# A new order and new engine choices for the tasks of an attention-then-SwiGLU kernel

## The chip, the cores and the metric

The kernel runs on one core of a Trainium2 chip. The metric is the device time of one execution in microseconds (us). Of the kernel before there are four timed executions, 257.27 to 258.35 us, with a median of 257.82 us, and one profiled execution of 259.26 us.

The core has a matrix engine (PE; its weight loads are listed as PEld), a vector engine (DVE), a scalar engine (ACT), a general engine (POOL) and a queue engine (SP), which issues the DMAs here. Each engine works through its own list of instructions in order. An instruction that needs another engine's result waits for it, and everything behind it on its engine waits too.

## The reference

```
# q, k, v: (4 batches, 8 heads, 768 positions, 64); heads 0, 2, 6 are "retrieval" heads
scores = q @ k^T / 8
retrieval heads: causal mask
other heads:     causal, and (key < 4  or  query - key < 64)
a = softmax(scores);  x = (a @ v), heads put side by side      # 3072 x 512
g = x @ w_gate;  silu = g / (1 + exp(-g))
out = (silu * (x @ w_val)) @ w_out                             # d_ff = 1536, float32
```

## The kernel before

The 3072 rows are 24 tiles of 128 queries. Tile t belongs to a pair n = t // 2, and a pair (256 positions of one batch, all heads) is what is loaded together: `load q n`, `load k n` and `load x n` (x is v), 512 KB each. The weights come in 18 loads of 512 KB: `load g n`, `load v n`, `load o n` with n from 0 to 5 for w_gate, w_val and w_out. All land as float32 in a ring of 14 buffers ("raw") and are cast to float16 by the tasks `cq`, `ck`, `cx` and `wc g`, `wc v`, `wc o` on ACT, DVE or POOL.

For pairs 0 to 4, q and k are turned on PE (`tr n.0` for q, `tr n.1` for k, lines 435 and 438) and copied out of PSUM by `evq` and `evk`. From pair 5 on, DMAs do that (`dq`, `dk`, lines 416 and 422). `fill3` clears the buffer that these DMAs read for q.

Each tile t then runs through: scores `sc t.u` on PE (line 547, one unit u after another through one PSUM buffer of two banks), exponentials `ex t.u` on ACT (line 557), and for tiles 4 and up a multiplication of units 0 and 1 by a 0/1 mask, `mask t.u`, on DVE or POOL (line 565; unit 0 has 128x1024 elements, unit 1 has 128x640). Then the values `val t.1` and `val t.0` on PE (line 577), and the division by the row sums, `nm` (lines 582 and 594). `sk` and `sv` copy the first four keys and values of a batch into other blocks. The tile is turned by PE (`xtr`, copied out by `xe`) for tiles 0 to 7, by a DMA (`xdma`, line 604) from tile 8 on.

Four tiles make a group g for the second half. For each of 12 slices j of d_ff, `gate g.j` and `vals g.j` (line 778, four matmuls each; the first four slices of group 0 are cut into two halves of columns, named .0 and .256) write to a ring of three PSUM banks ("gv"). `tanh` on ACT (line 784), `stt1` (line 788) and `stt2` (line 795) on DVE make h from them; `stt1` frees the gate's bank, `stt2` the value's bank. Slices 2n and 2n+1 need `wc g n` and `wc v n`. The output `out g.tt.third` (line 813) goes through one PSUM bank for groups 0 to 4, is copied out by `oe`, and stored by `st`.

All of that is recorded as a list of tasks, in the code's own order, with what each depends on. What is issued, and in which order, is written out by hand in two strings. `ORDER` holds two characters per task, a number in base 62: a number below 3700 is the index of a task in that list, and 3700 + k stands for k matmuls of a dummy product, `warm(k)` (line 292). `WAYS` holds one digit per task: which of the engines that the task allows is taken. Since every engine works in order, `ORDER` fixes each engine's list, SP's list of DMAs among them, and which PSUM or SBUF buffer is free for whom.

```
numbers = [DIGITS.index(ORDER[2 * i]) * 62 + DIGITS.index(ORDER[2 * i + 1]) ...]
for t, w in zip(self.tasks, WAYS):
    t.way = t.ways[int(w)]
...
for number in P.order():
    if number < P.FILL:
        P.tasks[number].run()
    else:
        warm(number - P.FILL)
```

Of the kernel before, what the change touches and what calls it, by code (L numbers as in the profile page):

```python
# [13 lines left out]


ORDER = (
    "000802041L1M1T091O1V1Nxl1Y1W1U1Z1X1a0A01xj1b1c0B1p1t1q0C1Q0E1R1P1r031f0D1d2527262D280i1u1s1S1y2G"
    "0j2j1g2E1exi1i1h1n2H1o212I2F1j2A1k1l1v221z2J2K1w1x201mxh2L2M23290F24xh2p2N2O2P2q2V2W2r2Q2R102B9F"
    "2C2S9G159j2X2Z9Z2a112k0p2s169k2b9H0H2t2Y2c2d9a9b9P2x9l2e2T2y3Q9m9c2U2h9n0o2u2i9Q2v369R0I0k9o9d9p"
    "05063W3Y0G133A129q9I9J9S9T3B0q9r9s3D073X3E9K9L9M3R3Z3a9N30319e3C0K189O9t3M3b9f9y0n2w2m2l9u9g9v3c"  # L20
    "329h3e33192z9zA0A10L499i3F349U2o354F0t3f2n3G0l0JA29w1H2fAN3d9V3p0m9W4A4G4H9x3H1I0s3h37AO3IAS3J3i"
    "383KAT3t3u9XAP394I3L9YAQ4J3j3k1B3SA83N3V4K0r0M3O3g3TAR3lAV1E3m4L0NAUA9AA3zAW3n3oAI403wAJAD3xA30O"
    "3P41421F3q3U3v43AK443r3sALAEAFAM0v4NA41C3y45461K4WA54p4O4qAG4oAHA60PA747480yAB4Z4yBk4a2gACBlBmBn"
    "4PBVBoBWBG4c4wAwBXBHBI4d0xAzAx4Q4RAyB00u4BBfBgBhBiBjBJBK4M4C4S4TBQBR4xB6B7BS4v0w4f4gAu4E0zB8BTAr"
    "0R4l4DAs4z5014BUAtB1B24U4V0S17AX4YAv52Ba53Bb4uB31D1ABYAY0Y4b4e4X5D1G4r4h5758B90QBZ4i5G1JAZ5W5X5Z"
    "4jAaBABLB45e515H5JBM5V5K544kBc0TAc4mB5BB555IAdAe5f4s59BN5LBC56BO5M5N5cAf5d0U5A5BAhAi5O5P5C5E4t5Y"
    "5Q5RBEBPAg5g635F5S5h5iAjAk5r4nBDBd0X5T5U62615a5s5tAmAnAoBFCd5b6iAbCeAp6ABeCgCfCh69CYCZCOBpCPCQ5o"
    "5y6B68Aq0WBqBrCa5jBsCRCS5p6F6GC9CbCcCA5k5qBuCB0V0a6C6DCs6O6HBvCt6X6Y5uCu6h6l6gAl6m5vCvCw6UCiBt66"
    "6V6o6p5l6n5m64CjCkCl6q6E6RCJ6SCK6d5w5xCLCECm6I6J6TBw655n5zD26K0h8d600ZCT7PBx7XByBzCF6WD30b6u6v67"
    "6LC07W6MD46P6NCMCUCNCV6Q6r6sC16Z6aC2C3D5CHD66x6y6bCG6eCW757TCICx6cCX7879Cn7OCC6j6k7BC46t71Cy0gC5"  # L30
    "C6C7CzCDD0Co726fEA0d7C7N7V7UEBD7Cp0cCqCr6z70D1C8D86w737AEF747v8283EC7REGEH7g7hE0E57jE6E17tE27u7k"
    "D9DAEIEJE77D767I7J0f7SEDEEE8E97Q7EDgDR7FDhDSDT7GDCDD7H7YE37K7L0e7Z8a8h7lDEDiDbDeE481DcDU807i7q87"
    "7mDdDFDG88EKDH7nDV8YDy77DI7a7bDfDJDvDK7cELEMDLDw847o7pDMDxDq858A8B7rDW8G7z8c8MDNDO8Z8NDz7s7MDrDs"
    "DPDtDu868P8i7dDjDk7eDX8fDZ8QDYDa7w8JENEODl7x8gDm8CEPDnDo7fFSDpFTDB8D8KFU8V89FIFJ8EF3FL8pFKEyFMEz"
    "F0EQERES8H8F8eF1F88qF28OF9FA8mFDFEF4EU8L7y8R8S8nEVETF5DQFVFW8j8xF6F78kEW8lEX8r8s8T8U8WFGFFFH8oFc"
    "FdFNFOFP93948IEZEaFf8b8tEY8u90FeFg8X91EtEuEbEcEvFQ8vFB8w8z8y92EwFC989A99FXExFY969BEeFZ97Eo95Ep9C"
    "Fa9D9EFbEfEqEgEhFRErEsEjEkEmElEnGuGvGwGBGxGyFhGGGHGIEiGCGDGkGlGmFiGnGoFjGEGFGQFkGRGsFmFnGpGSEdGq"
    "GrGtFoFpFqG1G2GVGWG4G3G5G6GXFrFsGYGZGaGbGcFtFuGJGKG7GLGMFwFlG8FvG9GdGAFxGTGNGeGUGOGPGfFyGgFzGhGi"
    "GzH0GjH1G0H4H5H6H9HAHBHEHFHGH7H2H3H8HCHDHJHHHIHKHL"
)  # L40
WAYS = (
    "000000000000000000000000000000000000000000000000000000000000002022222222222222222210201212101000"
    "011000000100000000000000010001100202212210110100100001000000000000000200022220001101000000000000"
    "020000000000000010012220220000000100000000000100000000100000000012210220110000100000000011000100"
    "000000021010210210000000000000000002000010000000000002200120000000100000000001000010001210200000"
    "001001000000200001000000000000222020100000010010000000021000000100000000020122000000001000000000"
    "010000210020002200000000010000000200010000000000101222022000000100000000000000001000000000000000"
    "000000000000000000000000000000000000000000000000000000000000000000000000000000000000010000000000"
    "000000000000000000000000000000000000000000000000000000000000000010000000001000000000000000000000"
    "000000000000000000000000000000000000000000000000000000000000000000000000000000000000000000000000"  # L50
    "000000000000000000000000000000001000000000100000000000000000000000000000000000000000000000000000"
    "000000000000000010000000000000000000000000000000000000000000000000000000000000000000000000000000"
    "10000000000000000010"
)
# [878 lines left out]
```

## Time and profile before

| | |
|---|---|
| median of four timed executions | 257.82 us |
| the profiled execution, its own time | 259.26 us |
| its span, first to last instruction | 257.1 us |
| mean granted clock of the matrix engine | 0.999 |
| PE busy | 247.3 us, 1813 matmuls |
| DVE busy | 167.6 us, 344 instructions |
| ACT busy | 139.3 us, 230 instructions |
| POOL busy | 97.3 us, 124 instructions |
| read from HBM, written to it | 28.31 MB, 6.29 MB |
| 128x512 matmul, four of them in a row | 0.86 us |
| mask 128x1024 on POOL, mean of both forms there | 1.88 us |
| mask on DVE, mean of both forms there | 0.74 us |
| exponential 128x1024 on ACT | 1.02 us |
| `stt1`, `stt2` on DVE, mean | 0.655 us |

The span is shorter than the time by 2.2 us, which lie before the first and after the last instruction. Busy time of PE counts a matmul from its start to its modelled end, so overlapping matmuls look longer than their share: a 128x512 matmul is listed with 368 ns, and yet four of them follow each other in 0.86 us.

### The profile page before, as it was taken

To read this page: it belongs to the slowest core of one execution; us is meant where nothing else is said; L and a number is where in the kernel's file an instruction comes from. 1 tells how busy PE (TensorE), PEld (TensorE's weight loads), DVE (VectorE), ACT (ScalarE), POOL (GpSimd) and SP (SyncE) were. 2 spreads that over 40 slices of the span, in tenths; PEclk is the share of its full clock that TensorE was granted. 3 is DMA by queue.
4 is the path that set the end of the run, shared out by engine and by line. 5 is a ranking of instruction groups with operands and counts; after the bars stand their busy time and mean duration, and the time that the engine had idled before them with its cause. 6 is when DMAs were issued, how large, how long until landed. Compare 5 with 4: busy or idle time off the path is not lost.

```text
span 257.1 us, 4866 instructions
## 1 busy us (share of the span) xinstructions
PE 247.3 (96%) x1813; PEld 136.8 (53%) x1813; DVE 167.6 (65%) x344; ACT 139.3 (54%) x230; POOL 97.3 (38%) x124
## 2 busy tenths in 40 slices
PE   7988988999999999999999999999999999999994
PEld 3666755765555564555655555555455554444442
DVE  3577999899869482588865637476665856455610
ACT  2876997776566664376655753564545323133101
POOL 6474689665661644263620821412142200000000
PEclk9999999999999999999999999999999999999999
DMA  7999999976958989997999972362222122031034
GB/s 186 290 320 317 318 324 333 288 248 157 323 148 204 224 161 192 236 220 158 223 231 233 182 163 55 70 129 59 60 56 50 20 55 49 0 83 41 16 94 97
DMA packets 80535, 42.52 MB, mean 165 GB/s; under 512 B 32768, under 2 KB 76032, under 8 KB 80512
## 3 DMA queue, kind: packets, MB, share of 16 engines
q1 hardware_dynamic: 80352, 42.09, 68.4%
q8 instruction: 14, 0.23, 0.4%
q10 hardware_dynamic: 160, 0.13, 0.2%
q14 instruction: 9, 0.07, 0.1%
HBM read 28.31 MB, written 6.29 MB: 135 GB/s over the span
## 4 chain that ended last, share of the span: by engine, by line
PE 78%; DVE 9%; SPq 5%; DMA 4%; ACT 2%; issue 1%; POOL 0%; DVEq 0%
PE gv L778 42%; PE o_ps L813 23%; PE sc L547 7%; PE av L577 4%; SPq L317 4%; DMA raw<-in_k_dram 4%; DVE h L795 2%; DVE e L565 2%; DVE vt L181 1%; DVE sil L788 1%; DVE xb L594 1%; SPq L325 1%; DMA out_dram<-o_sb 1%; ACT e L557 1%; ACT qT L175 1%
## 5 line engine op out<-in xcount | busy, mean ns | idle before, releaser
L557 ACT ACTIVATE e<-sc 128x1024 f16<-128x1024 f32 (+3 forms) x71 | 62.3, 880 | 35.3 <-PE sc L547 35.1
L778 PE MATMUL gv<-xt,wg_sb 128*128 128x512 f16 (+1 forms) x304 | 72.6, 368 | 1.0 <-POOL hq L177 0.6
L778 PE MATMUL gv<-xt,wv_sb 128*128 128x512 f16 (+1 forms) x304 | 72.6, 368 | 0.4 <-DVE sil L788 0.3
L813 PE MATMUL o_ps<-wo_sb,h 128*128 128x512 f16 (+2 forms) x300 | 70.0, 371 | 0.0
L788 DVE SCALAR_TENSOR_TENSOR sil<-sig,gv 128x512 f32<-128x512 f32 (+1 forms) x76 | 49.3, 655 | 30.9 <-ACT sig L784 30.1
L784 ACT ACTIVATE sig<-gv 128x512 f32<-128x512 f32 (+1 forms) x76 | 43.0, 575 | 48.5 <-PE gv L778 47.4
L795 DVE SCALAR_TENSOR_TENSOR h<-sil,gv 128x512 f16<-128x512 f32 (+1 forms) x76 | 49.2, 655 | 15.0 <-PE gv L778 13.8
L565 POOL TENSOR_TENSOR e<-e,m 128x1024 f16<-128x1024 f16 (+1 forms) x19 | 35.8, 1882 | 42.0 <-ACT e L557 37.7
L813 PEld LDWEIGHTS <-h 128*128 128x128 f16 x300 | 28.2, 98 | 28.4
L778 PEld LDWEIGHTS <-wg_sb 128*128 128x128 f16 x304 | 28.6, 98 | 27.6 <-issue 1.6
L778 PEld LDWEIGHTS <-wv_sb 128*128 128x128 f16 x304 | 28.4, 98 | 27.1 <-issue 0.9
L547 PE MATMUL sc<-qT,kT 128*128 128x256 f16 (+1 forms) x276 | 37.5, 257 | 0.1
L547 PEld LDWEIGHTS <-kT 128*128 128x128 f16 x276 | 25.2, 98 | 14.8 <-DVE kT L177 0.8
L577 PEld LDWEIGHTS <-e 128*128 128x128 f16 x472 | 19.8, 97 | 9.2 <-DVE e L565 1.7
L577 PE MATMUL av<-vt,e 128*128 128x65 f16 x472 | 22.5, 193 | 1.5 <-DVE e L565 0.7
L175 ACT COPY o_sb<-o_ps 128x512 f32<-128x512 f32 (+1 forms) x17 | 9.8, 579 | 20.5 <-PE o_ps L813 20.5
L594 DVE TENSOR_TENSOR xb<-av,rc 128x256 f16<-128x256 f32 x45 | 19.1, 424 | 1.5
L582 DVE RECIPROCAL rc<-av 128x4 f32<-128x4 f32 x48 | 8.6, 178 | 14.7 <-PE av L577 14.2
L177 POOL CAST vt<-raw 64x512 f16<-64x512 f32 x22 | 14.3, 651 | 9.3 <-DMA raw<-in_v_dram 8.4
L177 POOL CAST hq<-raw 128x1024 f16<-128x1024 f32 (+1 forms) x14 | 12.9, 927 | 10.5 <-DMA raw<-in_k_dram 6.8
L565 DVE TENSOR_TENSOR e<-e,m 128x640 f16<-128x640 f16 (+1 forms) x19 | 14.0, 740 | 0.2 <-ACT e L557 0.2
L177 DVE COPY o_sb<-o_ps 128x512 f32<-128x512 f32 (+1 forms) x8 | 5.1, 639 | 13.4 <-DMA out_dram<-o_sb 10.7
(55 smaller groups left out, 135.6 us busy)
## 6 DMA issues: line engine op xcount, KB each, us to landing
raw<-in_q_dram SPq DMA_DIRECT2D x12, 512.0 KB, 6.5
raw<-in_k_dram SPq DMA_DIRECT2D x12, 512.0 KB, 7.2
raw<-in_v_dram SPq DMA_DIRECT2D x12, 512.0 KB, 7.1
out_dram<-o_sb SPq DMA_DIRECT2D x46, 128.0 KB, 2.4
raw<-in_moe_w_gate_dram SPq DMA_DIRECT2D x6, 512.0 KB, 7.5
raw<-in_moe_w_val_dram SPq DMA_DIRECT2D x6, 512.0 KB, 8.1
raw<-in_moe_w_out_dram SPq DMA_DIRECT2D x6, 512.0 KB, 5.3
xt<-xb SPq DMA_TRANSPOSE x16, 2.5
```

The lines of the kernel that those rows point to most:

```text
L175: nc.scalar.copy(out=dst, in_=src)
L177: ENG[task.way].tensor_copy(out=dst, in_=src)
L547: nc.tensor.matmul(sc[c // 4][:, c % 4:c % 4 + n, :], weights, moving, start=first, stop=last)
L557: nc.scalar.activation(out=e[:, 0:n], in_=whole_sc.pop((t, u))[:, 0:n], func=AF.Exp, scale=scale)
L565: ENG[task().way].tensor_tensor(out=ev, in0=ev, in1=mm, op=ALU.mult)
L577: nc.tensor.matmul(av[:, n, 0:65], ee, vv, start=(m == 0), stop=(m == len(bl) - 1))
L594: nc.vector.tensor_tensor(out=xbs[t][:, :, odd, :], in0=av[:, :, 0:64], in1=rc.to_broadcast([128, 4, 64]), op=ALU.mult)
L778: nc.tensor.matmul(ps, wsb[:, kk, j * 128:(j + 1) * 128], xt[:, kk, c[0]:c[1]], start=(kk == 0), stop=(kk == 3))
L784: nc.scalar.activation(out=sg[g, j, c], in_=gs[g, j, c], func=AF.Tanh, scale=0.5)
L788: nc.vector.scalar_tensor_tensor(out=sl[g, j, c], in0=sg.pop((g, j, c)), scalar=1.0, op0=ALU.add, in1=gs.pop((g, j, c)), op1=ALU.mult)
L795: nc.vector.scalar_tensor_tensor(out=hs[g, j][:, c[0]:c[1]], in0=sl.pop((g, j, c)), scalar=0.5, op0=ALU.mult, in1=vs.pop((g, j, c)), op1=A ...
L813: nc.tensor.matmul(o_open[g, tt, x], hs[g, j][:, tt * 128:(tt + 1) * 128], wo_sb[:, j, lo:hi], start=(j == 0), stop=(j == NJ - 1))
```

## The change

The change replaces both strings and nothing else. The tasks, what they compute and what they depend on stay. Cut to its first lines:

```diff
 ORDER = (
-    "000802041L1M1T091O1V1Nxl1Y1W1U1Z1X1a0A01xj1b1c0B1p1t1q0C1Q0E1R1P1r031f0D1d2527262D280i1u1s1S1y2G"
...
+    "080400091L1O021M1N01xh1T1U1W1V1Xxi1Y1a1Z1K0B0A1Rxm1t1u25261P0C280E031Q2D1r2G1S1s271n1d1o1b2E2j2I"
...
 WAYS = (
-    "000000000000000000000000000000000000000000000000000000000000002022222222222222222210201212101000"
...
+    "000000000000000000000000000000000000000000000000000000000000002020222122002102002000012221100010"
...
```

Decoded, the engines' lists differ from place to place. PE's list from its start:

```diff
-warm(10) tr0.0 warm(5) tr0.1 warm(3) sc0.0 sc1.1 sc1.3 sc1.2 val0.1 sc0.1 tr1.0 val1.0 warm(2) val0.0
-sc1.0 tr1.1 xtr0 val1.1 warm(1) sc2.0 xtr1 warm(1) tr2.0 val2.1 sc3.0 val2.0 gate0.0.0 gate0.3.0 sc3.1
-val3.1 gate0.2.0 tr2.1 ...
+warm(10) warm(1) tr0.0 warm(2) tr0.1 warm(6) sc1.3 tr1.0 sc1.2 sc1.0 sc0.1 sc0.0 tr1.1 val0.0 val0.1
+sc1.1 sc2.0 val1.0 tr2.0 val1.1 sc3.0 warm(1) val2.1 xtr0 sc3.1 val3.1 xtr1 warm(1) val2.0 tr2.1
+gate0.2.0 ...
```

SP's list of DMAs from its start:

```diff
-q0 k0 x0 q1 k1 q2 x1 g0 g1 k2 v1 q3 v0 k3 g2 x2 v2 q4 g5 k4 v5 g3 x3 g4 v4 v3 x4 q5 k5 o1 x5 o4
-dk5.1 dq5.1 o3 o0 dk5.0 dq5.0 o2 o5 k6 x6 xdma8 ...
+q0 k0 q1 x0 k1 q2 x1 k2 g1 g0 v1 q3 v0 k3 g2 x2 v2 q4 g5 v5 g4 v4 x3 g3 k4 q5 v3 k5 x4 q6 o3
+dq5.0 dk5.0 dq5.1 dk5.1 k6 o2 o1 o4 o0 o5 xdma8 dk6.1 x5 ...
```

128 tasks go to another engine. By engine, the tasks whose numbers change:

| tasks | before | after |
|---|---|---|
| masks | DVE 19, POOL 19 | DVE 22, POOL 16 |
| casts of q and k | ACT 9, DVE 5, POOL 21 | ACT 6, DVE 7, POOL 22 |
| casts of v | ACT 16, DVE 10, POOL 22 | ACT 12, DVE 12, POOL 24 |
| casts of the weights | ACT 1, POOL 19 | ACT 8, DVE 2, POOL 10 |
| copies of turned k | ACT 3, DVE 4 | ACT 1, DVE 6 |
| copies of the output | ACT 17, DVE 8 | ACT 14, DVE 11 |
| divisions | ACT 3, DVE 45 | ACT 1, DVE 47 |
| copies of turned x | ACT 2, DVE 6 | ACT 1, DVE 7 |
| `fill3` | POOL | DVE |
| dummy matmuls on PE | 22 | 21 |

Of the first masks, 4.0 and 5.0 go from DVE to POOL, 6.0 from POOL to DVE, 6.1 and 7.0 from DVE to POOL; 4.1 and 5.1 stay on DVE and 7.1 on POOL. The two casts of the first q (`cq0.0`, `cq0.1`), which stood on ACT and POOL, both stand on ACT. Of the w_out casts, 1 and 3 go to DVE, 2, 4 and 5 to ACT, and 0 stays on POOL.

More of the change, by code (lines that the diff above doesn't have):

```diff
@@ L16 @@
 ORDER = (
-    "000802041L1M1T091O1V1Nxl1Y1W1U1Z1X1a0A01xj1b1c0B1p1t1q0C1Q0E1R1P1r031f0D1d2527262D280i1u1s1S1y2G"
[L18 to L36, printed above, removed]
@@ L37 @@
-    "Fa9D9EFbEfEqEgEhFRErEsEjEkEmElEnGuGvGwGBGxGyFhGGGHGIEiGCGDGkGlGmFiGnGoFjGEGFGQFkGRGsFmFnGpGSEdGq"
-    "GrGtFoFpFqG1G2GVGWG4G3G5G6GXFrFsGYGZGaGbGcFtFuGJGKG7GLGMFwFlG8FvG9GdGAFxGTGNGeGUGOGPGfFyGgFzGhGi"
-    "GzH0GjH1G0H4H5H6H9HAHBHEHFHGH7H2H3H8HCHDHJHHHIHKHL"
+    "080400091L1O021M1N01xh1T1U1W1V1Xxi1Y1a1Z1K0B0A1Rxm1t1u25261P0C280E031Q2D1r2G1S1s271n1d1o1b2E2j2I"
+    "2F1e2H1i1c1f2K1p0D1q292A2J2L1g0F1y2p2k1h1j2M2C2r2q1v0j1w1k151x2V2Wxh2N1z202O2P0i0p1l2B1m2X2Z2a23"
+    "242b2Yxh2Q2s9Z2R2S2c2t2T2d210H2U9j11309k312e9l109F0o2h2u9G162i9o9a9H9c2v0I0k0G9b9d3Q059e062x9f9p"
@@ new lines @@
+    "9q9m3W2y369n3D3Y9K0q9g22072z129I3E3X9J2f9N9L9M3A3B3M3R3Z3a9O189h2l2m9t9u9i2w3e9v9y0K329P333f9z9r"
+    "9s34A00n350t3b2n37199w9x2o3C0m3cA13F3G1H3H3IA249134FAN3J4G9QAO9R3h9S9T3i3K1IAQ3g3pAP1E3z0s401FAS"
+    "4HAR3d9UAV0J3S3TATAUAW3N9V3t380l3L3VAI0L9W3u1BAL3vAJ393j3k3l3mAKA8AM4A410N3n9X3o0r0O9Y3q4I423wA9"
+    "3xA34o0M3U434J44ADAA4N3r4p3y3sAG453OAEAF0Q2g1CA44O4K4WABAH4q463P4L4BA54748A64Z4aBQ4MACA70xBTBR4c"
+    "4l4dAwAx4vBS4CBU4xBf4PBg4DAyBh4Q4RBVBWAzBXB0ArAsB14bAtBiBj4S4w4TB24y5253B3B44U4VBGBH4z50B5BJBL5V"
@@ new lines @@
+    "0RBI4f0w5WBY4X4E4hBK5X1AB64gB75D4e5G5H0v17BZ1D510yB80u14BkAX5J4iB9BA0zBl4Y4j1J5K5fAY0PBM1GBNBm55"
+    "4m564r54BaBEAZAa4k5L5d4s594t4u575A5cAu585B5E5eBb5g5hAvAc0T5CAdBc0bAe5I5Q5MBO0SBP5Z0UBB5N5O5RAfBC"
+    "BDAhBd5P0VAi5S5TAjAb5oBFAk5pBnBeAg625Y634n64Bo5FAmAn5iAo5UCJ6761ApCd7SCKCL5r5s5tCeCf6BCgCh6ACsBp"
+    "Bq5q5a68COCtCu5j7T5k695yAq656F5bCv5u7Q0X6i5v6GCPCQAlBr0W6g6CBs0a6O6p5w5x6DCwC95lCACB6ECMBuCR6UCS"
+    "BvCNBwCn6V6I6hCoCpCb0Z6J6oBx6qBt0Y5zCY6kCZCaCcCT6X665m6Y6nBzCi6K6R6S7P0e6HC0C1Cl6LCjCkCmCCCUCV6M"
@@ new lines @@
+    "6d7W6uCD0g6T5n6v6NCE6P6w7XC260CHCxCFCGCI6rC46s7N6mC5Cy6z706Z6aCW6jCXCz6W6b6xCqC36QD08a6y7x6c6fCr"
+    "6eC6C7By7O7VD2757U6tD37RD1787971D5D47AEF72E0E1E20c73D67B7C0hD7EDD876EGC87j7kEHEIEJEAEBECD9DA7D7g"
+    "7t8i7l0d7vDRDB82DgDC7hEE7i7E7477DhDiE37m7n7z7FE5DSDTE6DDDEDF837GE47wE8Db7H6l7uE7E98eDUDVDcEK7I7Y"
+    "7JENELEM7qEO7Z7aDHDIDd7KDe7LDq80817o0fDrDs7p877rDfDJ7yDKDWDXDYDt7b7cDu88DlDm847sDo8GDnDp857d8ZDv"
+    "Dw8A7e8BDx89Dy8Y7MDM8JDG8KDjDzDk8LDN8MDZ7fEoEp8NFDFEDa868V8CFG8D8P8Q8c8E8gEqEjFFDOFH8dDPEkFIElDL"
@@ L40 @@
+    "EmFJ8f8h8pFL8FFKFMF88H8REP8qF9FA8jEn8k8bEQ8SEyEzFBERFC8m8lESETFS8xF0Et8nF18OEu8T8U9394F2EvEUEV8I"
+    "ErEw8W8t8X90FTFUFcEW8oEx918r8uFdFe92FfEXDQ8sFX8v8wFg8y98EZFYEYEaFZ9996EsF3F495F58zEbEc979AF6FN9B"
+    "9C9DEeEfF7FOFPFaFbFVEgFW9EGGEhGJEiGHGIGKGkGlGuGvGnGwGmFhFQGoGxGyFRG6G7FiFjFkFlEdG8GVGWGYGXGaG9Gb"
+    "GcGZFmGpFnGqGrG1G2GAG3GsGBGtGCGdGeGDFoGLGMFpG4G5GQFrGRGSFsGTFtGOFuGNGfGgFvGPFqFwGhGEGFFxFyFzG0GU"
+    "GiGzGjH0H1H4H2H3H5H6H7H8H9HAHBHEHFHCHDHGHHHJHIHKHL"
 )
 WAYS = (
-    "000000000000000000000000000000000000000000000000000000000000002022222222222222222210201212101000"
@@ L43 @@
[L43 to L52, printed above, removed]
@@ L53 @@
-    "10000000000000000010"
+    "000000000000000000000000000000000000000000000000000000000000002020222122002102002000012221100010"
+    "001000000000100000000000000000101221222020011101100000000000000000000110022100001101001000000000"
+    "100000100000000000002222220000100000100000000010000100100000000002022220110100000100000020000000"
+    "100000010012202210000001001000000000100000010000000002221202000000000000000001000010022211210000"
+    "000000000000220000001000000110202022000000000000000000000000000000000000012122000000000000000000"
@@ new lines @@
+    "010000210002221100000000010000001200010010000002001120011000000000000000000210000000000000000000"
+    "000000000000000000000000000000000000000000000000000000000000000000000000000000000000000000000001"
+    "000000000000000000000000000000000000000000000000000000000000000000000100001000000000000000000000"
+    "000000000000000000000000000000000000000000000000000000000000000100000000000000000000000000000000"
+    "000000000000000000000000000000000000010000100001000000000000000000000000000000000000000000000000"
@@ L54 @@
+    "000000000000000000000100000000000000000000000000000000000000000000000000000000000000000000000000"
+    "10000000001000000010"
 )
```

## The prediction

> **What bounds the kernel now.** I read the stages first: busy time of each engine in chosen stretches (busy us, then instructions).
>
> ```profile
> 0.00:15.00 15.00, 12.87 (x92) 6.91 (x92) 7.06 (x17) 9.30 (x19) 8.41 (x27) 1.00 0.99 246
> 15.00:30.00 15.00, 12.95 (x150) 10.21 (x151) 11.75 (x35) 10.99 (x22) 9.64 (x15) 1.00 1.15 321
> 30.00:45.00 15.00, 13.44 (x134) 8.90 (x133) 14.58 (x29) 12.62 (x22) 13.14 (x17) 1.00 1.13 328
> 45.00:120.00 75.00, 74.97 (x587) 42.34 (x584) 56.74 (x116) 48.11 (x76) 39.63 (x40) 1.00 0.88 213
> 135.00:257.00 122.00, 118.17 (x744) 60.11 (x742) 65.94 (x126) 50.25 (x81) 20.60 (x21) 1.00 0.38 80
> ```
>
> The columns are PE, PEld, DVE, ACT, POOL, granted clock, DMA share and GB/s. From 45 us on PE is full; no order can gain there but by leaving work out. Before 45 us it isn't, and from 30 to 45 us DVE is busy 14.58 of 15 us, POOL 13.14.
>
> I count PE's useful work by start-to-start times of matmuls in rows without waits: 216 ns for 512 columns, 109 for 256, 56 for 128, 29 for 65. Gates and values (544 x 216 + 64 x 109) are 124.4 us, outputs 62.2, scores with their mask terms 28.1, values of attention 13.8, transposes 6.3: 235 us, the same before and after. What the schedule decides is the **lag**: time minus useful work done. It is 10.2 us at 15 us, 13.9 at 30, 16.8 at 45, and 18.2 at the last matmul's start (253.1 us); 4.0 us of copy and store end the span. So 16.8 us are lost in the first 45 us (1.4 before the first matmul, 4.8 of dummies, 10.8 of waits), 1.4 in the other 208.
>
> Then who made PE late, in the waits from 18 to 46 us (total, times, longest):
>
> ```profile
> POOL hq L177 <- DMA raw<-in_k_dram: 2.5, 2, 1.9
> PEld L577 <- DVE e L565: 1.7, 2, 0.9
> PEld L435 <- POOL hq L177: 1.1, 1, 1.1
> ```
>
> Two causes: a late k (k2 landed at 22.0 us; tr2.1 needs its cast), and masks. The timelines of DVE and POOL show the masks:
>
> ```profile
> 32.78 0.69 DVE L565 TENSOR_TENSOR e<-e,m 128x1024 f16<-128x1024 f16 x1
> 33.72 1.75 DVE L565 TENSOR_TENSOR e<-e,m 128x1024 f16<-128x1024 f16 x1
> 36.87 1.24 DVE L565 TENSOR_TENSOR e<-e,m 128x640 f16<-128x640 f16 x1
> 38.96 1.48 DVE L565 TENSOR_TENSOR e<-e,m 128x640 f16<-128x640 f16 x1
> 40.91 0.68 DVE L795 SCALAR_TENSOR_TENSOR h<-sil,gv 128x512 f16<-128x512 f32 x1
> ```
>
> ```profile
> 32.31 1.62 POOL L177 CAST vt<-raw 64x512 f16<-64x512 f32 x2 [0.83 <-DMA raw<-in_v_dram]
> 33.89 1.03 POOL L177 CAST wv_sb<-raw 128x1024 f16<-128x1024 f32 x1
> 36.73 1.04 POOL L177 CAST wg_sb<-raw 128x1024 f16<-128x1024 f32 x1 [0.36 <-DMA raw<-in_moe_w_gate_dram]
> 37.73 2.37 POOL L565 TENSOR_TENSOR e<-e,m 128x1024 f16<-128x1024 f16 x1
> ```
>
> A DVE mask takes 0.69 us (128x1024) or 0.49 (128x640, at 47.43 us) when POOL is quiet. These three took 1.06, 0.75 and 0.99 more, ending about 0.35 us or more after a POOL instruction's end: they waited for it. That is 2.8 us on an engine with 0.4 to spare. At 41.64 us gate0.10 waits 0.65 us for a bank that the `stt2` of 40.91 frees.
>
> **The change, part by part.** I follow the lag at checkpoints, taking landings in order, each engine's list in order, and rows' durations (1.02 for a 1024 exponential, but 0.92 from start to start in a row; 0.60 likewise for a 512 `stt`).
>
> *Landings.* Up to q5 the loads land one after another, about 1.8 us apart for q, k, v and 1.53 for weights; so a load's place gives its time. k2 goes from the tenth place to the eighth: about 17.7 us instead of 22.0 (1.2 us of that is a delay before k2, which I leave in, behind it, for g1, g0 and v1). g0 gets later (17.4 to about 22), k4 38.4 to 46.3, x4 49.6 to 53.1. Their users moved too: gate0.0 behind val3.0, tr4.1 to 34.7 us of useful work (29.0 before).
>
> *The start.* Both halves of q0 are cast on ACT, 2 x 0.62 in a row instead of side by side: tr0.0 ends about 0.1 later. k0 is then cast on DVE and POOL at once, at 6.9: tr0.1 at 7.6 instead of 8.12. `fill3` on DVE isn't in the trace: by the 0.485 us of a 64x512 memset, twice as long a row gives 0.97; POOL's 1.8 is the other bound. It lies at 8.6, before v's landing at 10.5, so 1.9 us cover it; beyond that the cast of x0 is late. One dummy fewer is 0.2 us in a wait: nothing. Walking on, sc2.0 starts near 14.7 (15.8 before) and tr2.1 near 21.1, held now by xe1 behind an exponential and a v cast on ACT, not by k2. Useful work ahead of it is 8.75 us: lag 12.4, against 23.1 - 10.05 = 13.1. **Gain 0.7** there.
>
> *22 to 31 us.* v1 lands near 23.5 and is cast by 24.6; the gates' banks come free one by one: vals0.2.0 at 25.35, lag 13.1. Then ACT is the chain: ex4.1, evq3.10, ex5.1, evq3.00, five pieces of 0.92 to 1.02 from 27.15, end near 30.9; tr3.1 needs the last. 30.95 - 16.79 = 14.2, the same as before (31.27 - 17.06). **The gain is spent**: the ACT chain takes the place of the late k.
>
> *31 to 46 us, the masks.* DVE keeps 4.1 and 5.1 here, gets 6.0 (near 46, when POOL waits for ex7.0) and gives 4.0, 5.0, 6.1 and 7.0 to POOL. Removed from DVE: 0.69 + 0.69 and the stretch of 1.06. Mask 4.1 starts near 30.3, with ck3 and wc g2 on POOL from 29.3 to 31.35: between 0 and 1.05 late. 5.1 starts at 39.25, when wc v5 ends and mask 6.1 (1.39) begins: 0 to 1.4. Behind each on DVE stand the `stt2` that frees a bank, and PE behind that. POOL gets 2 x 2.12 and 1.39 more, and gives wc g5, g3, g4 (3.1) to ACT: val4.1 waits for mask 4.0 (31.35 to 33.5) and is due at 34.0, val5.1 for 5.0 (36.7), due at 38. Covered, by 0.5 and 1.3. Without any stretch: gate0.4.0 lag 14.2, gate0.10.0 14.9 (before 16.6), vals0.11.0 15.4 (before 16.9). With both in full: 15.0, 15.0, 16.8. I take the middle of the last pair, 16.1: **gain 0.8**, ends 0.1 and 1.5.
>
> The Trainium skill, "SBUF — State Buffer", section "SBUF: two separate sides", calls the port that DVE and POOL share an exclusive lock: whichever starts first has it "for the whole instruction". By that the mask of 33.72 would have waited for the cast ending at 33.94 and finished at 34.6; the trace shows 35.47, one more cast later. By the page mask 4.1 costs at most 1.05; by the row it can lose another turn.
>
> *SP.* dq5.0 is ahead of five w_out loads and waits for q5's casts (53); dk5.0 waits for k5's cast on POOL, near 57, behind masks. The loads are issued from 61 to 64 and land by 73 (before: by 71.1). out0.0.0 is due near 76 and needs wc o0 on POOL, after mask 10.0: 75.2. Cover 0.8. x5, now behind xdma8 and dk6.1, lands near 77, cast by 80; val10.1 is due at 82. The stores and xdma keep their neighbourhood; gate2's first xdma11 has no load just ahead of it any more (before it landed 0.14 us ahead of its use).
>
> *Later.* I summed DVE's work over stretches of 6 us of PE work. Before, the worst is 7.2 at 102 to 108, and PE's waits at 119 and 130 us (0.2, 0.4) lie around it; after it is 6.3 there, 7.1 at 54 to 60 (two w_out casts, by the tensor_reduce row about 1.2 each, if scaled; POOL 7.4), 6.2 at 78. Three gates' banks cover about 1 us of that. Of the 1.4 us lost late I take 0.3 as gained; ends 0.9 gained (the waits at 119, 130, 202) and 1.0 lost.
>
> *Sum*: 0.8 + 0.3 = 1.1 us off a span of 257.1, 256.0; with the 2.2 around it 258.2, against the profiled 259.26. The median is 257.8: **256.7** for the median after. The extremes: -1.5 - 0.9 gives 255.4; -0.1 + 1.0 gives 258.7.
>
> **Rivals.** *No change*, 257.7: both masks are stretched in full, lag 16.9 as before. For it: all three masks that met POOL work in the trace were. Against: three met it there, two do now. *A larger gain*, 255.3: neither is stretched and the late waits go (-2.4). For it: DVE has 1.4 us less to do from 30 to 45; against: ACT's chain leaves no reserve at 31. *Slower*, 259.3: mask 4.1 loses its turn twice, like the mask of 33.72. Then wc g2 is followed at 31.35 by mask 4.0 (2.12), and 4.1 ends near 33.9, not 31.8: 2.1 us more in front of stt2 0.0.0, which frees vals0.2.256's bank, and PE stands. On top of the stretched case (lag 16.9) that leaves about 1.5 once DVE's idle pieces are used: 257.7 + 1.6. It decides as soon as 4.1 ends later than about 32.8. For it: the row at 33.72; against: 36.87 and 38.96 lost one turn only.
>
> **How the numbers follow.** Forecast 0.33, larger gain 0.14, no change 0.23, slower 0.30. Less than 0.3% (0.8 us) can't be told from no change here. The two gains are faster: 0.47; same 0.23; slower 0.30. The range goes from 255.0, under the larger gain, to 259.2, nearly the slower rival; the forecast's own is 255.4 to 257.4.
>
> **What would show it.** tr2.1 near 21 us rather than 23.1; tr3.1 near 31 with ACT named; masks 4.1 and 5.1 under 1.5 us each; gate0.10.0 before 40.5 us; no PE wait over 0.5 us after 50. The prediction is wrong if lag at 45 us isn't below 16.8, if out0.0.0 waits for POOL near 76, or if DVE piles up at 71 to 77.

## The result, and the profile after

The kernel after takes 257.32 us (median of 44 executions, 256.67 to 258.10), the kernel before, on the same chip, 257.93 us (63 executions, 256.97 to 260.25). The ratio, which is that of the means, is 0.9966, 95% interval 0.9954 to 0.9977: faster by 0.3%. The medians differ by 0.6 us (0.24%). The profiled execution of the kernel after takes 257.32 us, too, with a span of 255.5 us; that of before took 259.26. Executions of the kernel before fall in two groups, 47 up to 258.35 us and 16 from 259.2 to 260.25, and its profile was taken of one in the upper group; so the 1.9 us between the two profiles are not the gain. The experiments look for where the groups come from.

The stages of the kernel after (columns as before: PE, PEld, DVE, ACT, POOL, clock, DMA share, GB/s; the last stretch ends 2 us earlier):

```profile
0.00:15.00 15.00, 12.15 (x87) 6.68 (x88) 8.62 (x19) 8.00 (x14) 8.42 (x27) 1.00 0.98 244
15.00:30.00 15.00, 13.41 (x162) 10.79 (x160) 11.96 (x38) 11.85 (x22) 9.84 (x17) 1.00 1.15 322
30.00:45.00 15.00, 14.23 (x134) 9.34 (x134) 13.81 (x34) 13.71 (x21) 12.93 (x11) 1.00 1.13 326
45.00:120.00 75.00, 74.75 (x579) 41.72 (x578) 58.16 (x115) 44.70 (x69) 32.83 (x41) 1.00 0.94 220
135.00:255.00 120.00, 116.79 (x741) 59.68 (x738) 72.49 (x133) 47.59 (x78) 10.60 (x13) 1.00 0.38 83
```

From 30 to 45 us PE is busy for 14.23 us instead of 13.44, while DVE does more instructions (34, not 29) in less time (13.81, not 14.58). What makes PE wait (total, times, longest), first in the kernel before from 16 to 46 us, then in the kernel after from 16 to 50 us:

```profile
PE tr L435 <- POOL hq L177: 0.8, 1, 0.8
PE av L577 <- DVE e L565: 0.7, 2, 0.4
PE gv L778 <- POOL hq L177: 0.6, 1, 0.6
```

```profile
PE sc L547 <- ACT e L557: 0.8, 3, 0.3
PE av L577 <- DVE rc L582: 0.4, 1, 0.4
PE av L577 <- DVE xb L594: 0.4, 1, 0.4
PE gv L778 <- DVE sil L788: 0.3, 1, 0.3
PE tr L435 <- ACT qT L175: 0.3, 1, 0.3
```

Neither the late k (`hq`) nor a mask (`e` of DVE) is in the second list; the exponentials (`e` of ACT) are. The masks themselves, on DVE and, with the casts around them, on POOL:

```profile
30.08 0.48 DVE L565 TENSOR_TENSOR e<-e,m 128x640 f16<-128x640 f16 x1
...
38.49 1.09 DVE L565 TENSOR_TENSOR e<-e,m 128x640 f16<-128x640 f16 x1
```

```profile
30.23 1.23 POOL L177 CAST wg_sb<-raw 128x1024 f16<-128x1024 f32 x1 [0.48 <-DMA raw<-in_moe_w_gate_dram]
31.43 2.12 POOL L565 TENSOR_TENSOR e<-e,m 128x1024 f16<-128x1024 f16 x1
...
38.20 1.04 POOL L177 CAST wv_sb<-raw 128x1024 f16<-128x1024 f32 x1 [0.60 <-DMA raw<-in_moe_w_val_dram]
39.21 1.64 POOL L565 TENSOR_TENSOR e<-e,m 128x640 f16<-128x640 f16 x1
```

Mask 4.1 (30.08) begins 0.15 us before the cast wc g2 (30.23) and takes 0.48 us; here the cast waits and takes 1.23 instead of 1.04. Mask 5.1 (38.49) begins inside a cast and takes 1.09.

### The profile page after: what moved, and what is told of

Read it like the earlier page. It is cut to its first block, busy times and chain, and to the rows that moved or that the text cites. A ratio compares the mean times of both kernels' runs of the same rounds, so it can differ in the third digit from the quotient of the medians.

```text
span 255.5 us, 4847 instructions
## 1 busy us (share of the span) xinstructions
PE 246.3 (96%) x1812; PEld 136.4 (53%) x1812; DVE 177.2 (69%) x360; ACT 135.3 (53%) x214; POOL 81.3 (32%) x118
## 4 chain that ended last, share of the span: by engine, by line
PE 84%; DVE 6%; DMA 3%; ACT 3%; SPq 2%; issue 1%; POOL 1%; DVEq 0%; POOLq 0%; ACTq 0%
PE gv L778 44%; PE o_ps L813 24%; PE sc L547 9%; PE av L577 5%; DMA raw<-in_k_dram 3%; ACT e L557 2%; SPq L317 2%; DVE h L795 1%; DVE sil L788 1%; DVE xb L594 1%; DVE vt L181 1%; DVE e L565 1%; ACT qT L175 1%; DVE qT L177 1%; PE xtr L610 0%
## 5 line engine op out<-in xcount | busy, mean ns | idle before, releaser
L778 PE MATMUL gv<-xt,wv_sb 128*128 128x512 f16 (+1 forms) x304 | 73.5, 368 | 0.4 <-DVE sil L788 0.3
L565 POOL TENSOR_TENSOR e<-e,m 128x640 f16<-128x640 f16 (+1 forms) x16 | 26.2, 1640 | 33.2 <-ACT e L557 31.5
L547 PEld LDWEIGHTS <-kT 128*128 128x128 f16 x276 | 24.6, 98 | 12.3 <-issue 1.3
L175 ACT COPY o_sb<-o_ps 128x512 f32<-128x512 f32 (+1 forms) x14 | 8.1, 578 | 26.0 <-PE o_ps L813 26.0
L594 DVE TENSOR_TENSOR xb<-av,rc 128x256 f16<-128x256 f32 x47 | 19.9, 424 | 1.6
L177 POOL CAST vt<-raw 64x512 f16<-64x512 f32 x24 | 15.4, 643 | 16.7 <-DMA raw<-in_v_dram 15.7
L177 POOL CAST hq<-raw 128x1024 f16<-128x1024 f32 (+1 forms) x15 | 14.2, 952 | 16.2 <-DMA raw<-in_k_dram 14.8
L177 POOL COPY vt<-vt 2x330 f16<-2x330 f16 x14 | 6.3, 452 | 37.0 <-PE av L577 36.5
L565 DVE TENSOR_TENSOR e<-e,m 128x1024 f16<-128x1024 f16 (+1 forms) x22 | 14.8, 672 | 0.8 <-ACT e L557 0.8
```

The source lines that it names most:

```text
L175: nc.scalar.copy(out=dst, in_=src)
L177: ENG[task.way].tensor_copy(out=dst, in_=src)
L547: nc.tensor.matmul(sc[c // 4][:, c % 4:c % 4 + n, :], weights, moving, start=first, stop=last)
L565: ENG[task().way].tensor_tensor(out=ev, in0=ev, in1=mm, op=ALU.mult)
L594: nc.vector.tensor_tensor(out=xbs[t][:, :, odd, :], in0=av[:, :, 0:64], in1=rc.to_broadcast([128, 4, 64]), op=ALU.mult)
L778: nc.tensor.matmul(ps, wsb[:, kk, j * 128:(j + 1) * 128], xt[:, kk, c[0]:c[1]], start=(kk == 0), stop=(kk == 3))
```

## The experiments

Edits are given as task names. A plan is cut at sc9.0, which PE issues at 58 to 59 us. The lag (time minus useful PE work, as in the prediction) of the profiled execution of each:

| kernel | its time | k2 lands | longest of DVE's masks 4.0 to 6.1 | tr2.1 | tr3.1 | gate0.10.0 | sc9.0 | out5.0.0 |
|---|---|---|---|---|---|---|---|---|
| before | 259.26 | 21.98 | 4.0: 1.75 | 13.07 | 14.21 | 16.57 | 16.96 | 18.22 |
| before_again | 260.44 | 21.91 | 4.0: 1.75 | 13.01 | 14.15 | 16.49 | 16.88 | 19.39 |
| before_third | 260.25 | 20.56 | 4.0: 1.75 | 11.79 | 13.86 | 16.67 | 17.06 | 19.17 |
| after | 257.32 | 17.63 | 5.1: 1.09 | 12.29 | 14.23 | 14.30 | 15.66 | 16.69 |
| after_again | 258.67 | 17.89 | 5.1: 1.42 | 12.54 | 14.46 | 15.29 | 17.00 | 18.03 |
| early_after_late_before | 258.45 | 17.54 | 5.1: 1.18 | 12.20 | 14.12 | 14.19 | 15.67 | 17.72 |
| early_before_late_after | 257.40 | 20.68 | 4.1: 1.18 | 11.90 | 13.59 | 14.30 | 14.80 | 15.93 |
| a_masks_back | 259.75 | 17.61 | 5.0: 1.63 | 12.26 | 14.19 | 17.60 | 18.05 | 19.08 |
| b_k2_early | 266.63 | 17.65 | 5.0: 3.12 | 16.82 | 18.70 | 23.79 | 23.87 | 25.56 |
| b_masks_pool | 267.56 | 21.87 | 4.1: 7.53 | 12.96 | 14.10 | 24.52 | 24.59 | 26.72 |
| eb_k2_la | 266.35 | 17.60 | 5.0: 3.13 | 16.67 | 18.38 | 23.40 | 23.48 | 24.82 |
| a_mfill1_late | 257.46 | 17.61 | 5.1: 1.03 | 12.26 | 14.19 | 14.26 | 15.58 | 16.83 |
| a_mfill1_evq | 257.10 | 17.71 | 6.0: 1.02 | 12.37 | 13.84 | 13.93 | 15.03 | 16.46 |
| eb_masks_up | 259.38 | 21.97 | 6.1: 1.33 | 13.07 | 14.20 | 14.39 | 16.21 | 17.87 |

### Which half of the plan gains

Beside a copy of the kernel before (before_again), the halves were crossed:

```diff
 early_after_late_before
-ORDER and WAYS from sc9.0 on: new
+ORDER and WAYS from sc9.0 on: before
 early_before_late_after
-ORDER and WAYS up to sc9.0: new
+ORDER and WAYS up to sc9.0: before
```

> The kernel before, once more, for a second profile. Theory A (the plan makes the loss): the lag of PE (time minus useful matmul work) is 17.0 us at sc9.0 again and 18.2 us at the end, span 257.1. Rival B (chance makes it: in the profile of before a mask lost its turn): if this execution is one of the shorter ones, mask 4.0 on DVE ends within 1.0 us of its start, and the lag at sc9.0 is 16.0 us or less.

> New order and engines up to the task sc9.0 (58 us), from there the old relative order and engines. Theory A (the gain is made before 58 us, where the lag went from 17.0 to 15.7): ratio to before 0.997 to 0.998, lag at sc9.0 15.7, at the end near 16.9. Rival C (the late part brings it, by the waits at 119, 130 and 202 us that went): ratio 0.999 to 1.001.

> Old order and engines up to sc9.0, the new ones from there. Theory A: ratio 0.998 to 1.000, lag at sc9.0 as before, and 1.0 us or less added after it. Rival C: ratio 0.996 to 0.998.

Measured on one chip, with before at 258.23 us (35 executions, 257.31 to 260.54): before_again 257.96, ratio 0.9992 (0.9959 to 1.0024); the new early part alone 258.63, 1.0009 (0.9982 to 1.0036); the new late part alone 257.76, 0.9989 (0.9953 to 1.0025). Neither half alone can be told from before. The first half's ratio fits its Rival C, the second's its Theory A, so neither theory holds for both. The profile of before_again fell in the upper group, with lag 16.88 at sc9.0, and could not tell its A from B. The profiles say more. From sc9.0 to out5.0.0 the plans of before lose 1.26, 2.51 and 2.11 us, and 2.05 behind the new early part; the new late part loses 1.03 in both profiles of the kernel after, and 1.13 behind the old early part. Over all 14 profiles the old late part loses 1.26 to 2.51 us (six, mean 1.96), the new 1.03 to 1.66 (eight, mean 1.24). One late wait is in all three profiles of before: a turned x that lands too late, 0.4 us in the first, 0.6 in the second, and in before_third (weight loads of PE, 60 to 255 us; total, times, longest):

```profile
PEld L778 <- DMA xt<-xb: 1.2, 1, 1.2
```

No such line is in the kernel after.

The other half was a surprise: the old early part, run before the new late one, had lag 14.80 at sc9.0, 0.9 us *better* than the new early part and 2.2 better than in the profile of before, with the same instructions in the same order. Yet 3 of its 12 executions took 260.3 to 261.1 us. So the early plan of before seems to have two courses, and all three profiles of before itself show the bad one.

The hybrid's time is not as good as its lag, and the reason lies behind the last matmul. From the start of that to the end of the span the kernels before and after take 4.0 us; early_before_late_after takes 4.8, as the last store, issued at 251.51, lands after 2.85 us instead of 2.04. The two other kernels with the old early and the new late part, eb_k2_la and eb_masks_up, take 4.9 and 4.8. An 8 KB read of instructions at 252.80 falls among these stores; that it delays them is not shown. Without the 0.8 us the hybrid's profiled execution would be near 256.6 us (an estimate, 257.40 less 0.8), under the 257.32 of the kernel after.

### The masks' engine, in both orders

```diff
 a_masks_back (the kernel after)          b_masks_pool (the kernel before)
-mask4.0, mask5.0 on POOL                -mask4.0, mask5.0 on DVE
+mask4.0, mask5.0 on DVE                 +mask4.0, mask5.0 on POOL
```

> The new plan with masks 4.0 and 5.0 back on DVE, the order as it is. Theory A (the masks' places make the gain of 31 to 46 us): two masks of 0.69 us more on DVE, each stretched by up to 1.0 us by casts on POOL; lag at vals0.10.0 16 to 17 us instead of 15.1, ratio to before 0.999 to 1.002. Rival D (the order of gates and loads makes it, the masks' engine is secondary): lag at vals0.10.0 under 15.6, ratio 0.996 to 0.998.

> The plan before with masks 4.0 and 5.0 on POOL, all else as it was, k2 at its late place. Rival F (masks on DVE are the cause): the lag at sc9.0 falls to 15.0 to 15.7 even where k2 lands at 22.0. Theory E: POOL in order gets 4.2 us more ahead of cq4 and wc g5; PE waits for those, lag at sc9.0 16.5 to 18, ratio 0.998 to 1.004.

Measured: a_masks_back 259.63 us, ratio 1.0039 (1.0010 to 1.0068), all 12 executions from 259.49 to 261.39. In the new order these two choices are worth about 2 us of median, more than the whole gain of the change: a_masks_back is 1.4 us above before beside it, the kernel after 0.6 under it. The lag at vals0.10.0 is 17.6 us, more than Theory A allowed. b_masks_pool: 267.67 us, 1.0356 (1.0307 to 1.0405), against 257.86 for before beside it. In the old order the same two choices cost 10 us, far beyond what was expected. Its DVE and POOL:

```profile
37.80 0.42 DVE L594 TENSOR_TENSOR xb<-av,rc 128x256 f16<-128x256 f32 x1
38.15 7.53 DVE L565 TENSOR_TENSOR e<-e,m 128x640 f16<-128x640 f16 x1
45.60 0.68 DVE L788 SCALAR_TENSOR_TENSOR sil<-sig,gv 128x512 f32<-128x512 f32 x1
```

```profile
38.03 1.04 POOL L177 CAST hq<-raw 128x1024 f16<-128x1024 f32 x1
39.02 1.04 POOL L177 CAST wg_sb<-raw 128x1024 f16<-128x1024 f32 x1
40.02 2.11 POOL L565 TENSOR_TENSOR e<-e,m 128x1024 f16<-128x1024 f16 x1
42.08 0.31 POOL L177 COPY kT<-kT 128x8 f16<-128x8 f16 x2
42.34 1.03 POOL L177 CAST hq<-raw 128x1024 f16<-128x1024 f32 x1
43.32 1.03 POOL L177 CAST wv_sb<-raw 128x1024 f16<-128x1024 f32 x1
44.30 1.03 POOL L177 CAST wg_sb<-raw 128x1024 f16<-128x1024 f32 x1
45.28 1.54 POOL L177 CAST vt<-raw 64x512 f16<-64x512 f32 x2
```

Read both together: mask 4.1, 0.49 us of work, begins 0.12 us after a cast, and each POOL instruction is followed by the next without a pause. The mask ends at 45.68, 0.35 us after the one at 44.30 has ended. It lost its turn to the six rows behind that cast. PE waited 6.4 us for it, and its granted clock from 42 to 49 us was 0.52:

```profile
42.00:49.00 7.00, 3.26 (x29) 2.78 (x30) 6.92 (x9) 0.48 (x2) 6.88 (x10) 0.52 1.14 324
```

### The early k2 by itself

```diff
 b_k2_early (the kernel before), eb_k2_la (early_before_late_after): SP's list
-... g0 g1 k2 v1 ...
+... k2 g0 g1 v1 ...
```

> The plan before with one load moved: k2 goes out ahead of g0 and g1 (eighth place instead of tenth). Theory E (the kernel before has two courses: a 16 KB read by one DMA engine near 19 us makes k2 land at 22.0 or at 20.7 us, and masks that miss a turn on DVE turn that 1.3 us into 2.1): k2 lands at 17.7, tr2.1 starts by 21.5, masks 4.0 and 5.1 on DVE take 0.5 to 0.8 us, the lag at sc9.0 is 14.5 to 15.0 as in the one short course, and no timed run is above 259.0; ratio to all runs of before 0.993 to 0.997. Rival F (the masks are late whatever k2 does): lag at sc9.0 16.5 to 17.0, and a third of the runs still near 260.

> Old plan with k2 early up to sc9.0, the new plan from there. If the old early part is the better one once k2 isn't late (lag at sc9.0 14.8 against 15.7 of the new plan) and the new late part adds 1.0 to 1.1, the end's lag is 15.8, span 254.7, median 256.3 to 256.6, faster than the new plan by 0.2 to 0.4%. If the gain needs the whole new plan: median 257.3 or more.

A miss, twice. Seven of the 12 executions of b_k2_early took 259.6 to 263.4 us, 2.5 us more in the median than before, and the ratio is theirs, 1.0089 (1.0042 to 1.0136); five took 265.6 to 267.2, the profiled one (266.63) among them. Of the six of eb_k2_la four took 259.8 to 263.4, with a ratio of 1.0131 (1.0061 to 1.0202), the other two 263.82 and 266.35, the latter profiled. In the profile of b_k2_early k2 does land at 17.65 instead of 21.98, but the gates' weights behind it land later, and POOL's list still has their casts ahead of k2's:

```profile
19.28 0.61 POOL L177 CAST wg_sb<-raw 128x512 f16<-128x512 f32 x1 [1.65 <-DMA raw<-in_moe_w_gate_dram]
19.95 0.61 POOL L177 CAST vt<-raw 64x512 f16<-64x512 f32 x1
22.27 1.04 POOL L177 CAST wg_sb<-raw 128x1024 f16<-128x1024 f32 x1 [1.71 <-DMA raw<-in_moe_w_gate_dram]
23.26 1.04 POOL L177 CAST hq<-raw 128x1024 f16<-128x1024 f32 x1
```

The last line is k2's cast, 5.6 us after its data. PE waits 2.8 us for the one at 22.27, and runs at half speed afterwards:

```profile
22.00:29.00 7.00, 5.63 (x44) 4.55 (x45) 1.96 (x7) 1.79 (x3) 5.39 (x7) 0.51 1.15 315
```

This stretch at half speed loses 3.4 us (0.49 of 7) and alone brings the mean clock of an execution down to 0.987. Only three of the 12, the profiled one among them, lie below that (0.980 to 0.981), and six have 0.997 or more. What the shorter executions lose by was not profiled. So the new place of k2 alone is worth nothing, and costs 2.5 us or more; in the kernel after gate0.0, the casts and PE's order move with it.

### The kernel after again, and the race in it

> The new plan once more, beside the others on the same chip. Theory E: no second course, since k2 lands ahead of the 16 KB read and g0, which lands behind it, has time: all runs within 257.0 to 258.3, lag at sc9.0 15.6 to 15.7 again. Rival: single runs at 259 or more.

Measured: 257.40 us, ratio 0.9973 (0.9946 to 1.0000); ten of 12 executions from 257.17 to 257.51, and two, against the theory, at 258.6. The profiled one is one of these two, and shows what the prediction called "stretched in full":

```profile
30.32 1.26 DVE L565 TENSOR_TENSOR e<-e,m 128x640 f16<-128x640 f16 x1
39.49 1.42 DVE L565 TENSOR_TENSOR e<-e,m 128x640 f16<-128x640 f16 x1
```

```profile
30.20 1.04 POOL L177 CAST wg_sb<-raw 128x1024 f16<-128x1024 f32 x1 [0.41 <-DMA raw<-in_moe_w_gate_dram]
31.20 2.36 POOL L565 TENSOR_TENSOR e<-e,m 128x1024 f16<-128x1024 f16 x1
```

Mask 4.1 is now 0.12 us behind the cast, not 0.15 ahead. It takes 1.26 us instead of 0.48, mask 5.1, a microsecond later than in the first profile, meets POOL's mask 6.1 (39.17 to 40.57) and takes 1.42, and the lag at sc9.0 is 17.00 instead of 15.66.

### Taking the race away, and then the chain of ACT

DVE fills mask m0 (`mfill1`) just ahead of mask 4.1, though tile 12 is the first to read it. The second kernel also moves the evacuation that PE's tr3.1 waits for.

```diff
 a_mfill1_late (the kernel after): DVE's list
-... mfill1 mask4.1 stt2 0.0.0 ... stt2 0.6.0 ...
+... mask4.1 stt2 0.0.0 ... stt2 0.6.0 mfill1 ...
 a_mfill1_evq: the same, and
-evq3.00 on ACT
+evq3.00 on DVE, ahead of mask4.1
```

> The new kernel with one instruction moved: the fill of mask m0 (not read before tile 12) goes on VectorE from before mask 4.1 to after the second combination of tile 6. Theory (mask 4.1 races with wc g2 for the gap in GpSimd's stream: it started at 30.08 and 30.32 us in the two profiles of the new kernel, wc g2 at 30.23 and 30.20, and the loser took 1.26 us): without the fill before it the mask starts at 28.5 to 28.8 us, waits for ck3's end at 29.7 at most, is out by 30.2 in every execution, and the lag at sc9.0 is 15.2 to 15.7 us; no execution above 258.3, median 257.0 to 257.4, that of the new kernel or a little less. Rival (the race is only moved: mask 5.1 or the fill itself now meets a GpSimd instruction): lag at sc9.0 16.5 to 17.2, median 257.6 to 258.3.

> As the run before, and the last eviction of q tile 3's chain on ScalarE (evq3.00, on whose release tr3.1 stands for 0.46 us at 30.45) goes to VectorE ahead of mask 4.1. Theory (the early gain was spent on the chain of ScalarE that ends in evq3.00, as the prediction had it): tr3.1 starts at about 30.5 instead of 31.0, gate0.4.0 at about 31.25 (lag 13.6, now held by wc g2), lag at sc9.0 14.7 to 15.1, median 256.5 to 256.9. Rival (what is won at tr3.1 is lost again in the turns of VectorE and GpSimd, mask 5.1 first): lag at sc9.0 15.6 or more, median 257.3 or above.

Measured on one chip, with before at 258.17 (22 executions): a_mfill1_late 257.45 us, 0.9957 (0.9929 to 0.9985), all 12 executions from 257.26 to 257.79: the median stays, and no late execution is among them. Mask 4.1 starts at 28.72 and takes 0.48; lag at sc9.0 15.58. It still meets POOL: the cast ck3 starts at 28.72, too, and takes 1.38 us instead of 1.04. What a lost turn would cost there no profile shows. a_mfill1_evq **256.72 us**, 0.9925 (0.9897 to 0.9954), 256.50 to 257.22, the fastest kernel of this study, with every execution below all 12 of a_mfill1_late; lag at sc9.0 15.03. ACT in the kernel after, then in a_mfill1_evq:

```profile
29.05 1.02 ACT L557 ACTIVATE e<-sc 128x1024 f16<-128x1024 f32 x1
29.98 0.99 ACT L175 COPY qT<-tr 64x1024 f16<-64x1024 f16 x1
30.87 0.38 ACT L784 ACTIVATE sig<-gv 128x256 f32<-128x256 f32 x1
```

```profile
29.12 1.02 ACT L557 ACTIVATE e<-sc 128x1024 f16<-128x1024 f32 x1
30.04 0.38 ACT L784 ACTIVATE sig<-gv 128x256 f32<-128x256 f32 x1
```

The copy of 0.99 us (evq3.00) is gone from the chain; the tanh behind it runs 0.83 us earlier, and tr3.1 starts at 30.63 instead of 31.02. Not all of the gain is ACT's chain: mask 5.1, which took 1.03 us beside a POOL cast in a_mfill1_late, starts ahead of that cast here and takes 0.48. In the stage from 30 to 45 us PE is busy for 14.78 us, not 14.23:

```profile
30.00:45.00 15.00, 14.78 (x145) 10.04 (x144) 13.98 (x33) 13.06 (x21) 12.49 (x11) 1.00 1.12 326
```

### What splits the executions of before

My explanation after the first runs was k2: its transfer met a read of 16 KB of instructions in the profile of before (k2 at 21.98) and not in early_before_late_after (20.68).

> The kernel before once more, for a profile of its short course. Theory (two courses from one race: whether k2's transfer meets the 16 KB read of instructions): either k2 lands at about 20.7 and the lag at sc9.0 is 14.8 to 15.1 us, the profiled time below 258.4; or k2 lands at about 22.0, and the lag is 16.8 to 17.1 again. Rival (something else makes the two clusters): a lag of 16.8 to 17.1 with k2 at 20.7, or of 14.8 with k2 at 22.0.

The rival came true: k2 landed at 20.56, and the lag at sc9.0 was 17.06 all the same. The early tr2.1 (lag 11.79) was lost again. (k2's own landing does go with that read. Where it begins at 18.7 to 19.2 us, k2 lands at 21.9 to 22.0, in four profiles of this order; where it begins at 20.4 to 20.7, at 20.6 to 20.7, in two.) The masks of before_third, and then of early_before_late_after:

```profile
32.44 1.14 DVE L565 TENSOR_TENSOR e<-e,m 128x1024 f16<-128x1024 f16 x1
33.83 1.75 DVE L565 TENSOR_TENSOR e<-e,m 128x1024 f16<-128x1024 f16 x1
```

```profile
32.16 0.68 DVE L565 TENSOR_TENSOR e<-e,m 128x1024 f16<-128x1024 f16 x1
33.10 0.77 DVE L565 TENSOR_TENSOR e<-e,m 128x1024 f16<-128x1024 f16 x1
```

POOL's casts of v2 begin at 32.42 in the one and at 32.38 in the other. Mask 5.0 begins 0.02 us after them, or 0.22 before. In the first case it takes 0.46 more, mask 4.0 comes 0.73 later, into the casts that run to 35.03, and takes 1 us more still. In the profile of before there was another way to the same place: mask 5.0 began at 32.78, late already, took its 0.69, and mask 4.0 came at 33.72. What the three long profiles share is mask 4.0 beginning at 33.65 to 33.83 and taking 1.75; at 33.10 it took 0.77. The last run moves both masks ahead of these casts:

```diff
 eb_masks_up (early_before_late_after): DVE's list
-... mfill1 stt1 0.0.256 mask5.0 stt2 0.0.256 mask4.0 ... nm5.0 ...
+... mask4.0 mask5.0 stt1 0.0.256 stt2 0.0.256 ... nm5.0 mfill1 ...
```

> The earlier hybrid (order and engines of before up to sc9.0, the new plan from there) with three instructions moved on VectorE: masks 4.0 and 5.0 go to the place of the fill of mask m0 (30.2 to 30.8 us), and the fill goes behind the division of tile 5 (46 us). Both masks stay on VectorE. Theory (what makes the long executions of before is mask 4.0 meeting the casts of v2 on GpSimd at 33.1 to 34.9 us; in the hybrid it took 0.77 us, in three profiles of before 1.75): in their new place the masks meet at most wc g2 (30.1 to 31.1) and then find GpSimd idle until 32.3; both are out by 32.5, mask 4.0 takes at most 1.3 us, the lag at sc9.0 is 14.0 to 14.9 us, 15.2 to 16.2 at out5.0.0, the median 255.6 to 256.5, and no execution is above 258. Rival A (they lose their turns at wc g2 and the copies behind it, and the first combination stt1 0.0.256 is late): lag at sc9.0 15.0 to 17.0, median 257.2 or above. Rival B (the long executions come from elsewhere, a load's landing for one): both courses stay, about one execution in four lies some 2.5 us above the rest.

Half right. k2 landed late this time (21.97, lag 13.07 at tr2.1), the masks took 0.97 and 0.68, and at gate0.10.0 the lag was 14.39, where before has 16.57 with the same k2. So a late k2 alone does not make the 2.2 us. This run moved a fill of 1.4 us out of the stretch as well, so it does not show by itself that the masks' turns make them. Two other profiles show more, with k2 at 20.56 and 20.68 and the same order up to sc9.0: in before_third masks 4.0 to 5.1 on DVE take 5.60 us together, in early_before_late_after 3.31, and the lag at gate0.10.0 is 16.67 and 14.30, 2.3 us of masks beside 2.4 of lag. No execution fell in a second group that far off: all 12 lie from 258.65 to 259.68. But the median is 258.86, ratio 1.0016 (0.9991 to 1.0041), 2.4 above what I expected: the fill, put at 43.63 us, delays stt2 0.1.256 and mask 6.1, which at 46.29 meets the cast wc v4 of 46.23, takes 1.33 us, and PE waits for the `stt2` behind it; another 0.8 us are the late last stores told above. Its waits from 16 to 50 us:

```profile
PE gv L778 <- DVE h L795: 1.2, 2, 0.9
PE tr L435 <- POOL hq L177: 1.1, 1, 1.1
```

The fill was moved from one crowded place into another.

## Why the prediction was right, and where it was not

The forecast of 256.7 us was 0.6 under the 257.32 measured, and the direction held. By its steps:

- *Landings and the start*: right. k2 landed at 17.63 (said: 17.7), g0 at 22.04 (22); sc2.0 stood at 14.57 (14.7), tr2.1 at 21.05 with lag 12.29 (12.4). `fill3` took 0.91 us (0.97).
- *"The gain is spent"* at tr3.1: right, and tested. Lag 14.23 (14.2), and before had 14.21. a_mfill1_evq took a piece out of ACT's chain and won 0.4 us there; its median is 0.73 us under that of a_mfill1_late beside it, and mask 5.1 has a part in that.
- *The masks*: that masks and POOL's work hold each other up was right, and the size that I took was not. I took the middle of the stretched pair of ends, lag 16.1; measured 15.22 at vals0.11.0, close to the unstretched end (15.4). Mask 4.1 is 0.15 us ahead in the profile, and the times of 54 of the 56 executions speak for the same. The other end (15.0, 15.0, 16.8) is what after_again shows: 15.23, 15.29, 16.55. Both were right as ends; it is a choice between them from one execution to the next, not a middle. The trace of before had shown that masks can win, and I misread it. I said that all masks that met POOL work were stretched, and took the masks of 32.78 and 47.43 for ones with POOL quiet. Both met casts, and there the casts paid: the pair at 32.31 took 1.62 us, where the pair at 43.50 takes 1.27, and the one at 47.43 took 0.96 instead of 0.61.
- *Late part*: forecast a gain of 0.3 us. Between the two profiles it is 0.23 (1.26 against 1.03 lost), against the other two profiles of before 1.5 and 1.1. The fears did not come true: PE waits for nothing at out0.0.0 (75.47 us), with wc o0 done by 74.5, and though DVE is busy for 5.73 of the 6 us from 71 to 77, PE is busy for all of them.
- *The last step* was wrong: "with the 2.2 around it 258.2, against the profiled 259.26", and from there to the median. I carried the 1.4 us between the profiled execution of before and its median over to the new kernel as if it were fixed; they came from the course that this one execution had taken. The new kernel's profiled execution equals its median, 257.32. Nor was the time around the span fixed: it fell from 2.2 to 1.8 us. The gain between the profiles was larger than forecast (1.9 us, not 1.1), the gain between the medians smaller (0.6).
- *A small slip*: the parts of the early loss (1.4, 4.8 and 10.8 us) add up to 17.0, not 16.8.
- *The rivals*: "no change", both masks stretched in full, is after_again's profiled execution; it is the rarer course, and with 258.67 us it is 1 us above its price of 257.7, by the same fixed step from profile to median. "Slower", mask 4.1 losing its turn twice, did not happen in the two profiles of the kernel after, but its mechanism is real: in b_masks_pool mask 4.1 lost six.

The Trainium skill's lock of "SBUF — State Buffer", section "SBUF: two separate sides", fits the meetings with one POOL instruction: in after_again mask 4.1 ends 0.34 us after the cast it met, mask 5.1 0.34 us after POOL's mask. It does not tell of b_masks_pool's case, where the next POOL instruction ran before the waiting mask did, again and again; there the measurement decides.

Where the gain comes from: 0.4 us of it lie outside the span, where the prediction held 2.2 us fixed; that part of the gain is luck. Time less span is 2.15 to 2.33 us in all 110 executions of before whose span the experiments recorded, with a mean of 2.20, and 1.73 to 1.84 in the 56 of the kernel after, with a mean of 1.79. The cause stays open. In each profile of before an 8 KB read of instructions begins some 1.8 us after the last instruction (at 258.89 us in the first, whose span ends at 257.1), in none of the kernel after; b_k2_early and b_masks_pool, the only others with such a read, have 2.2 and 2.0 us, the remaining kernels 1.8 to 1.9.

The rest is that long executions became rare. The mean of all 63 executions of before is 258.24 us, that of the 47 in the lower group 257.74, that of the kernel after 257.35. So 0.5 us of the 0.9 between the means are the upper group, and the 0.4 to the lower group are those outside the span: inside it the new plan's usual execution is no faster than before's. By the profiles two parts cancel there. The new late part loses 0.7 us less (1.24 against 1.96, the means above), and the new early part is 0.9 us worse than before's good course (lag 15.66 against 14.80 at sc9.0). That good course is read from early_before_late_after alone; no profile of before itself caught it, so this balance is inferred. In the five comparisons on record 16 of 63, 13 of 35, 4 of 23, 6 of 22 and 6 of 17 executions of before were above 258.9 us; of the kernel after, none of 56. What decides, from one execution to the next, whether masks 5.0 and 4.0 of before come some tenths sooner or later stays open; k2's landing alone does not.

## What to carry to other kernels

Where DVE and POOL hold each other up, look in the profile for pairs that start within 0.2 us of each other, as mask 4.1 and its cast do (0.15 and 0.12 us): such a pair can be a race, of which one profile shows one outcome, while the executions' times show both. Look, too, at which of the two was stretched: a mask with its usual time may have won its turn. Price a forecast against the median with the profiled execution's place among the executions in view, not by a fixed offset, and compare the spans as well as the times: a difference outside the span shows in no wait and no lag. And a changed order or choice of engine is worth what its neighbours make of it: the same two masks on POOL gained about 2 us in one order and lost 10 in the other, and the early k2 lost 2.5 us or more without the moves around it.
